# K and V of the first head on GpSimd's queue, ahead of the zero fills, in a decode step with its gradients

## The chip, the cores and the metric

The kernel runs on one core of one Trainium2 chip. Its time is the device time in microseconds (us). A kernel's time is the median of several executions, with the fastest and the slowest in brackets. Each trace is of one profiled execution, and its span is that execution's length.

## The reference, cut to what matters

One token goes through a layer norm, an attention over the last 4096 positions of a cache of 32768, and a gated block. Then the gradients of all inputs are taken.

```python
# x [1,1,448]; k_cache, v_cache [1,8,32768,256]; wq [448,4096]; wo [4096,448]; all bf16
W = 4096                                      # only the last W cache rows take part
k = repeat(k_cache[:, :, Sk - W:, :], 2)      # 16 query heads on 8 cache heads
v = repeat(v_cache[:, :, Sk - W:, :], 2)
p = softmax((q @ k.T) * Dh ** -0.5);  o = p @ v
h  = x + o @ wo
h2 = h + (layernorm(h) @ w_gate * (layernorm(h) @ w_up)) @ w_down
# results: h2 and the gradients of x, k_cache, v_cache, wq, wo, w_gate, w_up, w_down
```

The gradients of the two caches are what costs. Each is 134 MB, and seven eighths of both are zeros, which have to be written.

## The kernel before

Three things go on beside each other. GpSimd's queue (q0 in the profile) writes zeros from a buffer of 16 KB per partition, in fills of 2.1 MB. SyncE's queue (q1) brings most weights and the K and V rows of each head, and takes the results away; ScalarE's (q10, 1.61 MB in all) brings the up weights of the block. The engines compute attention, then the block, then the gradients.

`LD` is SyncE's queue, `ZQ` is GpSimd's.

```python
zeros = ar(0, ZW)                                # ZW = 8192 elements in each partition
...
nc.vector.memset(ar(0, ZW // 2), 0.0)            # L96: VectorE clears the first half,
nc.gpsimd.memset(ar(ZW // 2, ZW // 2), 0.0)      # L97: GpSimd the second
...
LD.dma_start(out=wqA, in_=wq_A)                  # query weights, 3.67 MB with the next line
LD.dma_start(out=wqB, in_=wq_B)
LD.dma_start(out=x_bf[:], in_=A_x.rearrange("a b d -> (a b) d"))
...
send_fills(0, HALF0)                             # the first 42 fills read all of zeros
send_fills(HALF0, HALF1, True)                   # 15 more read only its first half
...
load_kv(K_off[0], A_k_cache, 0)                  # all on LD, 2.1 MB each
LD.dma_start(out=dh2_bc[:], in_=grad_out...)
load_kv(V_off[0], A_v_cache, 0)
load_kv(K_off[1], A_k_cache, 1)
load_kv(V_off[1], A_v_cache, 1)
```

The block is worked through in three parts of 640, 512 and 640 columns. Part 2's gate and up weights lie in the second half of `zeros`, so they can't be loaded before the first 42 fills have been read out. When part 2 is done, that half is cleared again and the remaining fills are issued. I call this the **refill**.

```python
wgu_off = [RB + 28 * KB, ZW // 2]                # parts 1 and 3 | part 2, in the second half of zeros
...
for n in range(len(BLOCKS)):
    ...                                          # gate, up, down of part n
    if n + 2 < len(BLOCKS):
        load_block(n + 2)
    if n == 1:
        nc.vector.memset(ar(ZW // 2, ZW // 2), 0.0)   # L443
        send_fills(HALF1, len(fills) - 1)             # the refill
...
late_jobs = [(out_2, G - 1, 5, 7, 2 * ZW), (out_3, G - 1, 0, 6, 2 * ZW), (out_3, G - 1, 6, 7, ZW)]
# SyncE's own zero fills, issued behind the last gradients' stores
```

## Time and profile before

| of the profiled execution | before |
|---|---|
| median time, before the change was tried | 793.55 us (793.19 to 794.0, 3 runs) |
| span | 791.1 us |
| bytes moved | 334.75 MB, on average 423 GB/s |
| busiest compute engine | PE, 60% of the span |
| first fill issued, then first packets of q0 | 5.13 us, then 10.82 us |
| attention's last head done, refill issued, last SyncE stores issued | about 314, 383.3 and 742.9 us |

How to read it: the bytes over the plateau rate set a floor, and what comes on top are holes, stretches in which the DMA engines moved less than the plateau rate. The last row gives places where compute hands work to the queues. If compute were the bound, moving those times would move the end. The prediction shows the lines of the page, the windows and the first microseconds. These are the lines of the stage with the refill, from the timeline (start in us, duration, engine, line, operation, and in brackets the idle time before and what ended it):

```profile
315.62 0.38 SPq L366 DMA_DIRECT2D arena<-in_B_w_gate_dram  x1
...
353.05 1.50 PE L420 MATMUL gu_ps<-X_b,arena 128*128 128x1 bf16 x18 [2.59 <-DMA arena<-in_B_w_up_dram]
...
370.39 0.28 PE L420 MATMUL gu_ps<-X_b,arena 128*128 128x1 bf16 x3 [8.03 <-DMA arena<-in_B_w_gate_dram]
...
383.29 5.71 POOL L142 DMA_DIRECT2D out_dram<-arena  x6 [30.72 <-DVE arena L443]
...
742.93 0.95 SPq L661 DMA_DIRECT2D out_dram<-arena  x2
```

Part 2's gate weights are issued at 315.62, and PE's gate and up matmuls of part 2 run from 350.25 to 356.4 us, most of them from 353.05 on. The line at 370.39 is part 3, after 8 us of waiting for part 3's gate weights, which were issued at 355.36. The refill goes out at 383.29, for which GpSimd (POOL) had waited 30.7 us. VectorE had waited too: its last step of part 2 (376.07) stands behind its first step of part 3 (375.63). The last pair of the gradients' stores is issued at 742.93.

### The profile page before, as it was taken

To read this page: it belongs to the slowest core of one execution; us is meant where nothing else is said; L and a number is where in the kernel's file an instruction comes from. 1 tells how busy PE (TensorE), PEld (TensorE's weight loads), DVE (VectorE), ACT (ScalarE), POOL (GpSimd) and SP (SyncE) were. 2 spreads that over 40 slices of the span, in tenths; PEclk is the share of its full clock that TensorE was granted. 3 is DMA by queue.
4 is the path that set the end of the run, shared out by engine and by line. 5 is a ranking of instruction groups with operands and counts; after the bars stand their busy time and mean duration, and the time that the engine had idled before them with its cause. 6 is when DMAs were issued, how large, how long until landed. Compare 5 with 4: busy or idle time off the path is not lost.

```text
span 791.1 us, 7239 instructions
## 1 busy us (share of the span) xinstructions
PE 475.9 (60%) x2926; PEld 220.8 (28%) x2926; DVE 410.6 (52%) x621; ACT 196.1 (25%) x309; POOL 29.8 (4%) x41
## 2 busy tenths in 40 slices
PE   0359998999999999453226848583551535363100
PEld 0224333344343433142114714231210211131000
DVE  2105764847658476052884288486680583555300
ACT  0043123141241301000101207372331344134300
POOL 6000000000000000110300000000000000001000
PEclk9987999999999999655556959886556556556555
DMA  9999999999999999999999999999999999999998
GB/s 345 429 432 430 429 430 431 432 431 432 428 427 430 427 427 426 418 420 422 433 431 425 425 425 432 427 429 430 427 426 429 428 427 429 423 428 407 413 439 350
DMA packets 28759, 334.75 MB, mean 423 GB/s; under 512 B 1966, under 2 KB 5046, under 8 KB 6966
## 3 DMA queue, kind: packets, MB, share of 16 engines
q0 software_dynamic: 15904, 216.01, 64.2%
q1 hardware_dynamic: 11382, 116.68, 35.1%
q10 hardware_dynamic: 1440, 1.61, 0.6%
q8 instruction: 23, 0.38, 0.2%
q14 instruction: 10, 0.08, 0.0%
HBM read 53.69 MB, written 280.59 MB: 423 GB/s over the span
## 4 chain that ended last, share of the span: by engine, by line
another core or an unknown queue 40%; DMA 25%; DVE 14%; PE 10%; issue 2%; POOL 2%; ACT 1%; DVEq 0%; ACTq 0%; SPq 0%; POOLq 0%
DMA out_dram<-arena 25%; DVE arena L469 2%; PE rows_ps L266 2%; DVE arena L658 2%; DVE arena L554 2%; PE dqb_ps L512 2%; DVE arena L659 2%; PE d_ps L651 2%; PE tr_ps L263 1%; DVE arena L524 1%; DVE arena L438 1%; POOL out_dram L138 1%; PE dqb_ps L515 1%; DVE arena L623 1%
## 5 line engine op out<-in xcount | busy, mean ns | idle before, releaser
L322 DVE TENSOR_TENSOR arena<-arena,p_f 128x2048 bf16<-128x2048 bf16 x64 | 145.4, 2287 | 64.3 <-PE M_ps L327 64.2
L327 PE MATMUL M_ps<-arena 128*128 128x512 bf16 x512 | 129.3, 381 | 0.2 <-ACT arena L333 0.2
L651 PE MATMUL d_ps<-arena 32*128 32x512 bf16 x256 | 45.4, 521 | 100.6 <-DVE arena L659 85.7
L263 PE MATMUL tr_ps<-ident_bf,arena 128*128 128x128 bf16 x1024 | 92.2, 241 | 20.2 <-DMA arena<-in_A_k_cache_dram 12.7
L266 PE MATMUL rows_ps<-arena,vpad 128*16 128x512 bf16 x256 | 89.5, 445 | 21.4 <-DVE arena L623 15.9
L263 PEld LDWEIGHTS <-arena 128*128 128x128 bf16 x1024 | 68.3, 107 | 74.2 <-issue 60.3
L280 ACT COPY arena<-tr_ps 128x1024 bf16<-128x1024 bf16 x64 | 61.8, 1015 | 70.5 <-PE tr_ps L263 70.5
L330 PE MATMUL ok_ps<-arena 128*16 128x512 bf16 x256 | 64.0, 381 | 0.9 <-DVE arena L307 0.9
L655 ACT CAST arena<-d_ps 128x512 bf16<-128x512 f32 x64 | 37.7, 589 | 106.1 <-PE d_ps L651 106.1
L327 PEld LDWEIGHTS <-arena 128*128 128x128 bf16 x512 | 43.3, 99 | 59.2 <-issue 23.4
L621 ACT COPY arena<-tr_ps 128x1024 bf16<-128x1024 bf16 x32 | 32.5, 1016 | 109.9 <-PE tr_ps L263 35.8
L658 DVE CAST arena<-d_ps 128x512 bf16<-128x512 f32 x64 | 43.9, 686 | 18.2 <-PE d_ps L651 17.7
L659 DVE CAST arena<-d_ps 128x512 bf16<-128x512 f32 x64 | 43.6, 681 | 15.5 <-DMA out_dram<-arena 15.5
L651 PEld LDWEIGHTS <-arena 32*128 32x128 bf16 x256 | 10.7, 96 | 126.0 <-issue 81.9
L656 ACT CAST arena<-d_ps 128x512 bf16<-128x512 f32 x64 | 38.1, 595 | 16.8 <-DMA out_dram<-arena 16.8
L266 PEld LDWEIGHTS <-vpad 128*16 128x16 bf16 x256 | 18.7, 91 | 58.4 <-issue 50.6
L330 PEld LDWEIGHTS <-arena 128*16 128x16 bf16 x256 | 19.1, 89 | 41.6 <-issue 20.5
L549 DVE TENSOR_SCALAR arena<-arena,xT 128x1792 bf16<-128x1792 bf16 (+1 forms) x9 | 7.7, 881 | 37.1 <-DMA out_dram<-arena 37.1
L295 ACT ACTIVATE e_f<-cols_ps,nbias 128x32 f32<-128x32 f32 x16 | 4.5, 286 | 86.9 <-DVE nbias L291 86.9
L524 DVE CUSTOM_DVE_ANT_0 arena<-arena 128x4096 bf16<-128x4096 bf16 x3 | 13.1, 4421 | 23.7 <-ACT arena L517 23.7
L268 DVE COPY arena<-rows_ps 16x512 f32<-16x512 f32 x16 | 10.8, 676 | 27.7 <-PE rows_ps L266 27.7
L623 DVE COPY arena<-tr_ps 128x1024 bf16<-128x1024 bf16 x32 | 21.8, 683 | 3.0 <-PE tr_ps L263 2.5
(198 smaller groups left out, 382.2 us busy)
## 6 DMA issues: line engine op xcount, KB each, us to landing
out_dram<-arena POOLq DMA_DIRECT2D x11, 14336.0 KB, 196.1
out_dram<-arena SPq DMA_DIRECT2D x18, 2048.0 KB, 25.6
out_dram<-arena POOLq DMA_DIRECT2D x15, 2048.0 KB, 54.2
arena<-in_A_v_cache_dram SPq DMA_DIRECT2D x10, 2048.0 KB, 52.8
arena<-in_A_k_cache_dram SPq DMA_DIRECT2D x8, 2048.0 KB, 31.3
out_dram<-arena SPq DMA_DIRECT2D x4, 4096.0 KB, 26.1
out_dram<-arena POOLq DMA_DIRECT2D x1, 12288.0 KB, 43.0
out_dram<-arena POOLq DMA_DIRECT2D x1, 8192.0 KB, 337.3
```

Source lines behind the costliest of these rows:

```text
L263: nc.tensor.transpose(tr_ps[:, dh, i, :], X_sb[:, 4 * q + i, dh * 128:(dh + 1) * 128], ident_bf[:])
L266: nc.tensor.matmul(rows_ps[:], lhsT=pad[:, dh, 16 * q:16 * q + 16], rhs=XT[:, dh].rearrange("p t k -> p (t k)"), start=(q == 0 and dh == 0 ...
L280: sT_ps = dots(kv_at(K_off[g]), KT_slot, vpad[g % 2], rows1, ps_c, "cols", lambda q, XT, ps: nc.scalar.copy(out=XT, in_=ps))
L322: nc.vector.tensor_tensor(out=pK, in0=K_sb[:, 4 * c:4 * c + 4, :].unsqueeze(2).to_broadcast([128, 4, 2, Dh]), in1=p_f[:, c::8, :].unsqueez ...
L327: nc.tensor.matmul(M_ps[:, vh, :], lhsT=V_sb[:, t, vh * 128:(vh + 1) * 128], rhs=pK[:, i, :, :].rearrange("p h d -> p (h d)"), start=(t == ...
L330: nc.tensor.matmul(ok_ps[:].rearrange("p k d -> p (k d)"), lhsT=ppad[g % 2][:, 8 * (t % 4) + t // 4, :], rhs=both(g, t), start=(g == 0 and ...
L621: nc.scalar.copy(out=XT, in_=ps)
L651: nc.tensor.matmul(d_ps[:, qi].rearrange("p w d -> p (w d)"), lhsT=rTm[32 * q:32 * (q + 1), l, :], rhs=R_sb[32 * q:32 * (q + 1), :], start ...
L655: nc.scalar.copy(out=stV[:, t:t + 2, :], in_=d_ps[:, :, 0, :])
L656: nc.scalar.copy(out=stK[:, t:t + 2, :], in_=d_ps[:, :, 1, :])
L658: nc.vector.tensor_copy(out=stV[:, t:t + 2, :], in_=d_ps[:, :, 0, :])
L659: nc.vector.tensor_copy(out=stK[:, t:t + 2, :], in_=d_ps[:, :, 1, :])
```

## The change

Its intent: GpSimd's queue lies idle while the zeros are cleared. If it carries K and V of the first head in that time, they no longer stand behind the query weights in SyncE's queue, nor ahead of head 1's K and V, and attention can start earlier. GpSimd must not clear zeros then, so VectorE clears both halves.

```diff
-    nc.vector.memset(ar(0, ZW // 2), 0.0)
-    nc.gpsimd.memset(ar(ZW // 2, ZW // 2), 0.0)
+    def load_kv(eng, off, cache, g):
+        eng.dma_start(out=kv_at(off), in_=cache[0, g, Sk - W:, :].rearrange("(p t) d -> p t d", t=T))
+
+    load_kv(ZQ, K_off[0], A_k_cache, 0)
+    load_kv(ZQ, V_off[0], A_v_cache, 0)
+    nc.vector.memset(zeros, 0.0)
...
-    load_kv(K_off[0], A_k_cache, 0)
     LD.dma_start(out=dh2_bc[:], in_=grad_out.rearrange("a b d -> (a b) d").to_broadcast([128, D]))
-    load_kv(V_off[0], A_v_cache, 0)
-    load_kv(K_off[1], A_k_cache, 1)
-    load_kv(V_off[1], A_v_cache, 1)
+    load_kv(LD, K_off[1], A_k_cache, 1)
+    load_kv(LD, V_off[1], A_v_cache, 1)
# ... every other load_kv gets LD as its first argument, and stays where it was
```

More of the change, by code (lines that the diff above doesn't have):

```diff
@@ L204, in layernorm_bwd @@
         return r
-    def load_kv(off, cache, g):
-        LD.dma_start(out=kv_at(off), in_=cache[0, g, Sk - W:, :].rearrange("(p t) d -> p t d", t=T))
-    load_kv(K_off[0], A_k_cache, 0)
     LD.dma_start(out=dh2_bc[:], in_=grad_out.rearrange("a b d -> (a b) d").to_broadcast([128, D]))
-    load_kv(V_off[0], A_v_cache, 0)
-    load_kv(K_off[1], A_k_cache, 1)
-    load_kv(V_off[1], A_v_cache, 1)
+    load_kv(LD, K_off[1], A_k_cache, 1)
+    load_kv(LD, V_off[1], A_v_cache, 1)
     dup = small.tile([1, 128], bf16, tag="dup", bufs=1)
@@ L237 @@
     nc.vector.tensor_copy(out=qT_bf[:], in_=qT_ps[:])
-    load_kv(K_off[2], A_k_cache, 2)
-    load_kv(V_off[2], A_v_cache, 2)
+    load_kv(LD, K_off[2], A_k_cache, 2)
+    load_kv(LD, V_off[2], A_v_cache, 2)
     pT_all = const.tile([128, G, T, 2], bf16)
@@ L347 @@
                 if kind == "K":
-                    load_kv(K_off[n], A_k_cache, n)
+                    load_kv(LD, K_off[n], A_k_cache, n)
                 else:
-                    load_kv(V_off[n], A_v_cache, n)
+                    load_kv(LD, V_off[n], A_v_cache, n)
             if g == G - 2:
@@ L518 @@
         for g in range(2):
-            load_kv(MB + 16 * KB * g, A_v_cache, g)
+            load_kv(LD, MB + 16 * KB * g, A_v_cache, g)
         HJ = H * Dh // 2
```

## The prediction

> **What bounds the kernel now.** I read the page's slices first, to see whether any engine or the DMA is full all the time. The digits are tenths of busy time in 40 slices of 19.8 us, then GB/s; q0 is the queue that GpSimd issues on, q1 that of SyncE.
>
> ```profile
> PE   0359998999999999453226848583551535363100
> DVE  2105764847658476052884288486680583555300
> DMA  9999999999999999999999999999999999999998
> GB/s 345 429 432 430 429 430 431 432 431 432 428 427 430 427 427 426 418 420 422 433 431 425 425 425 432 427 429 430 427 426 429 428 427 429 423 428 407 413 439 350
> ...
> q0 software_dynamic: 15904, 216.01, 64.2%
> q1 hardware_dynamic: 11382, 116.68, 35.1%
> ...
> HBM read 53.69 MB, written 280.59 MB: 423 GB/s over the span
> ```
>
> No compute engine is full except PE in slices 4 to 15. The DMA is full everywhere, and only the first slice, the last and two near slice 37 are visibly under the plateau. So the kernel is bound by moving 334.75 MB, nearly all of it zeros being written to the two cache gradients. At 432 GB/s, the rate of the window from 11 to 20 us below, those bytes take 334.75 / 0.432 = 775 us. The span is 791.1 us, so everything that is not plain streaming, at the start, at the end and in between, is 16 us in sum. That is the whole pot a reordering of transfers can win from: a gain of 2% (15.9 us) would need all of it.
>
> Then I read where these 16 us lie, in the windows view (last two columns: DMA share and GB/s; the first is the window).
>
> ```profile
> 2.00:4.00 2.00, 0.00 (x0) 0.00 (x0) 1.99 (x10) 0.03 (x1) 2.00 (x1) 1.00 0.82 262
> 4.00:8.00 4.00, 0.37 (x1) 0.09 (x1) 1.80 (x9) 0.00 (x0) 3.95 (x8) 1.00 1.02 422
> 8.00:11.00 3.00, 0.00 (x0) 0.00 (x0) 0.00 (x0) 0.00 (x0) 3.00 (x4) 1.00 0.93 243
> 11.00:20.00 9.00, 0.00 (x0) 0.00 (x0) 0.00 (x0) 0.00 (x0) 1.64 (x3) 1.00 1.01 432
> 742.00:744.00 2.00, 0.14 (x4) 0.00 (x0) 1.29 (x2) 1.07 (x2) 0.00 (x0) 0.50 0.80 331
> ```
>
> Lost against 432: about 2 us before anything flows; 2 x 170/432 = 0.8 us in 2 to 4; 3 x 189/432 = 1.3 us in 8 to 11; 2 x 101/432 = 0.5 us in 742 to 744. The rest is scattered (rates of 418 to 425 in slices 17 to 24) or is the end.
>
> Third, when GpSimd's queue starts to move anything: the timeline of the engines that clear the zeros, and the DMA queues within a window (packets, MB).
>
> ```profile
> 0.74 3.51 POOL L97 MEMSET arena<- 128x4096 bf16 x1 [0.29 <-POOLq L694]
> 5.13 6.07 POOL L142 DMA_DIRECT2D out_dram<-arena  x6
> 11.19 1.45 POOL L138 DMA_DIRECT2D out_dram<-arena  x2
> 71.02 0.68 POOL L138 DMA_DIRECT2D out_dram<-arena  x1 [58.38 <-DMA out_dram<-arena]
> ...
> 1.25 1.76 DVE L96 MEMSET arena<- 128x2048 uint32 x1 [1.25 <-PEq L694]
> ```
>
> ```profile
> q1 hardware_dynamic: 238, 1.95, 96.2%
> q0 software_dynamic: 3, 0.05, 1.9%
> ```
>
> The second fence is 5 to 11 us: q0 moved three packets, although its first fill was issued at 5.13. From 11 to 13 us it moved 41. So q0 begins about 6 us after its first issue, and until then q1 carries the query weights alone.
>
> Last, what the compute chain waits for at the start, in the waits of 20 to 60 us and the timeline:
>
> ```profile
> PE ps L171 <- DMA x_bf<-in_A_x_dram: 14.7, 1, 14.7
> ...
> DVE pad L223 <- DMA dh_bc<-in_grad_out_dram: 10.1, 1, 10.1
> ...
> 58.48 1.78 PE L263 MATMUL tr_ps<-ident_bf,arena 128*128 128x128 bf16 x15 [4.97 <-DMA arena<-in_A_k_cache_dram]
> ```
>
> PE waits for x (behind the weights) until 21.0, for K of head 0 until 32.2, for the output gradient until 37.9, for K of head 1 until 58.5; after that attention runs on to about 314.
>
> **What the Trainium skill says.** "DMA: Bandwidth & Descriptors", section "Issuing engines are not separate DMA queues": DMAs of all issuers run on the same 16 engines and interleave, and using more issuers saves only issue time. The trace agrees: 432 GB/s from two queues in 11 to 20 us, 422 from one in 4 to 8. The same page, "Queues, rings and completion order": an engine takes turns between queues at packet granularity. The trace agrees roughly: where both have large rows each queue gets half. "VectorE: DVE Perf Modes", section "Zero memsets can be issued as uint32 (trn2)": one cycle per element whatever the type, so zeros go as 4-byte elements. The trace shows it: 4096 bf16 as 2048 uint32 in 1.76 us, against 3.51 us on GpSimd. "SBUF — State Buffer", section "Who interferes with whom": a VectorE instruction outside the 2-port modes with at most one SBUF input doesn't contend with GpSimd. The memsets of before overlapped (1.25 to 3.01 beside 0.74 to 4.25); whether GpSimd's descriptor writing is left alone too, no run here shows yet.
>
> **The change part by part.**
> Zero clearing: VectorE's memset doubles, 2 x 1.76 = 3.5 us, from 1.25 to about 4.8. GpSimd loses 3.51 us and gains two DMA issues of about 0.7 us (the 2 MB issues at L138 take 0.68), so its two identities (0.9 us in sum) are done near 3.2. Then the first fill waits for the memset until 4.8: 5.13 becomes about 4.9. Off the bound, worth 0.2 us at most.
> Queue order: K and V of head 0 (2 x 2.10 MB) go from q1 to the head of q0. Bytes removed: none. Issued at about 0.75 and 1.5 and with the 6 us delay measured above, q0 starts at about 6.5 instead of 11.1, and the fills start behind 4.2 MB of loads.
> Compute: in q1 the weights (3.67 MB, packets of 8 and 4 KB against 16 KB of q0) share from 6.5 instead of 11 us, so x and q come about 4 us later, near 31. But K and V are there, and the output gradient and K of head 1 follow directly. K of head 1: 4.2 MB fewer in front at some 210 GB/s is 20 us earlier, less the 4 us of slower weights, so near 41. Scores of head 0 take 17 us (38 to 54 before), so 31 to 48, and head 1's start near 46 instead of 58.5. Attention, the block after it and the gradients can thus run up to 12 us ahead, perhaps 8 in the later stages, where stores queue behind fills.
> What that is worth: little. The work before each stage goes faster, but the bytes queue on the same engines. Compute 8 to 12 us ahead means that q1 has carried more at a given time and q0 less; the fills then last longer beside the last stores. Before, q0 was empty by 733 and q1 alone carried the last 23 MB. Afterwards the two end closer together, at the same total.
> Sum: start, of 1.3 us in 8 to 11 I take half, 0.6, because the dip may come with the starting queue and only move to 4 to 7 us; earlier fill, 0.1; ramp in 2 to 4 us, nothing, as q0 isn't there yet; the hole at 742 filled by remaining fills, 0.5; other holes of 710 to 750, 0.3. In all 1.5 us: 793.55 - 1.5 = **792.0 us**.
>
> **Rivals.**
> A, compute was the path: the 12 us head start comes through, 793.5 - 12 = 781. For it: the last stores and late fills (SyncE's) are issued only after the last gradient stage, at 743. Against: DMA digit 9 in all slices; ending at 781 would need 430 GB/s with hardly a loss.
> B, the fills become the end: q0 gets 4.2 MB more, the split between the queues was tuned, and q0 finishes later. If all of it came out unhidden, 4.2/0.432 = 9.7 us more: 803. Against: q0 was empty 58 us before the end, far more than it gains; its limit of transfers in flight is untouched too: the third 2 MB fill waits for the first large one at 71.02, eight issues earlier, and two loads more in front only make the first two such fills wait for K and V.
> C, a new wait: the gradients of the block overwrite half of the zeros, so compute that is early can be held until the first 42 fills have landed, which the loads ahead delay by bytes moved out of q1; that sum is the same at 305. It would eat the head start, not add time: 793 to 794. A quarter of the chances lies here or with a start dip that only moves.
>
> **Range and chances.** The bytes set a floor near 779 (775 plus the 2 us before any flow and 2 at the end), and I see no idle DMA that the change could open wider than a few us. The noise of before is 0.8 us. I take **788.5 to 795.0** as the range. Faster by over 2% means under 777.7, below the floor: 0.01. Slower by over 2% means 809.4, with some stall that I haven't seen: 0.015. Within 2%: 0.975.
>
> **What would show it.** Right: DMA digits and the plateau as before, 334.75 MB again, q0's first packets near 6.5 us, x later than 21 us, head 1's transposes near 46 instead of 58.5, the last gradient stage ending before 743, q0 not empty at 733, and no DMA dip there. Wrong: the mean rate moves by more than 0.5%; q0's first packets come after 8 us; a slice in the middle drops under 400 GB/s because GpSimd waits longer; or a stretch at the end with only some of the engines working.

## The result, and the profile after

The kernel after took **794.03 us** (793.64 to 794.31, 4 runs), against 793.49 us (793.19 to 794.0, 4 runs) of before in the same rounds. The ratio is 1.0006, with a 95% interval from 0.9988 to 1.0023: the same. Ratios here are the mean time of one kernel's fast runs over that of the other's of the same rounds, so not quite the ratio of the medians quoted beside them. The span of the profiled execution was 792.0 us.

The page after, its lines of rates (40 slices) and of queues (packets, MB, share):

```profile
GB/s 358 401 430 432 428 432 428 432 429 430 432 428 429 429 421 413 426 423 422 430 432 418 427 419 431 428 429 427 427 427 428 429 427 428 421 429 408 420 441 356
...
q0 software_dynamic: 16192, 220.20, 65.7%
q1 hardware_dynamic: 11094, 112.48, 33.8%
```

4.2 MB moved from q1 to q0, and the sum is what it was. The first slice gained 13 GB/s, and the second, 19.8 to 39.6 us, lost 28. So what the start won was given back at once. The windows of after (the last two columns are DMA share and GB/s) show where:

```profile
8.00:11.00 3.00, 0.00 (x0) 0.00 (x0) 0.00 (x0) 0.00 (x0) 3.00 (x4) 1.00 0.96 410
...
18.00:22.00 4.00, 0.00 (x0) 0.00 (x0) 0.00 (x0) 0.00 (x0) 0.00 (x0) 1.00 1.03 291
...
742.00:744.00 2.00, 0.61 (x4) 0.11 (x4) 1.29 (x3) 1.07 (x2) 0.00 (x0) 0.50 0.91 386
```

The dip of 8 to 11 us is gone (243 before, 410 now), but 18 to 22 us has one of 291 GB/s. It costs 4 x (432 - 291)/432 = 1.3 us, as much as the old one. The packets of the first fill come at 21.5 us, at the end of the new dip. Before, they came at 10.82, at the end of the old one. In neither dip are the engines idle for long: the DMA share is 0.93 in the old one and 1.03 in the new. The packets take longer. In before, q1's packets of 8 KB took 1.023 x 16 x 4 us / 206 = 0.32 us each in 4 to 8 us and 0.896 x 16 x 3 us / 83 = 0.52 us in 8 to 11 (share of q1, 16 engines, window, packets). The hole at 742 shrank from 331 to 386 GB/s, worth 2 x 55/432 = 0.25 us.

The start, in the timeline of after:

```profile
1.29 0.70 POOL L97 DMA_DIRECT2D arena<-in_A_k_cache_dram  x1 [0.84 <-POOLq L693]
...
1.67 3.47 DVE L101 MEMSET arena<- 128x4096 uint32 x1 [1.67 <-PEq L693]
...
5.44 5.82 POOL L146 DMA_DIRECT2D out_dram<-arena  x6 [1.95 <-DVE arena L101]
...
27.86 0.21 DVE L215 COPY dup<-x_bf 1x128 bf16<-1x128 bf16 x1 [21.47 <-DMA x_bf<-in_A_x_dram]
...
48.03 0.68 PE L262 MATMUL tr_ps<-ident_bf,arena 128*128 128x128 bf16 x9
```

K of head 0 is issued at 1.29 and V at 2.00. The whole memset takes VectorE 3.47 us, and the first fill is issued at 5.44 after waiting 1.95 us for it. x is there at 27.9 (21.0 before). A head has 64 transposes; the first of the nine at 48.03 is the 64th, so head 1's start at 48.1 instead of 58.5. The same 5 to 11 us by queues (packets, MB, share of packet time), in which q0 had moved three packets before:

```profile
q0 software_dynamic: 95, 1.56, 62.0%
q1 hardware_dynamic: 121, 0.99, 39.4%
```

So compute did get ahead. VectorE's multiplies for attention's moments (products of K and V weighted by p, behind a head's softmax) began at 56.2 us instead of 61.5, and the last ones ran at 292.4 instead of 304.8, which is 12.4 us earlier. The lead grew on the way: 9.1 us at the first multiplies of head 1 (81.1 against 90.2), 9.6 at head 2's, 12.4 at head 3's. The last step is a wait of PE for K, 2.72 us, which ended at 130.50 in before and has no counterpart in after. But now the refill's stage, in the timeline of after:

```profile
346.18 1.23 SPq L365 DMA_DIRECT2D arena<-in_B_w_gate_dram  x1
...
369.72 0.41 PE L419 MATMUL gu_ps<-X_b,arena 128*128 128x1 bf16 x3 [30.55 <-DMA arena<-in_B_w_gate_dram]
...
385.36 5.65 POOL L146 DMA_DIRECT2D out_dram<-arena  x6 [31.81 <-DVE arena L442]
...
743.53 1.58 SPq L660 DMA_DIRECT2D out_dram<-arena  x2
```

PE waits 30.55 us for part 2's weights and gets to them at 369.72, 19 us later than before (350.25). Part 3 now follows at once, at 377.97 (370.39 before). The whole lead has become a wait: the refill is even 2 us later, and the last stores are 0.6 us later. The two traces differ in the order of SyncE's issues. Before, part 2's gate weights were issued at 315.62 and 321.82, ahead of part 3's. After, the build put part 3's loads first in SyncE's and ScalarE's queues, and part 2's gate weights went out at 346.18. Part 3's loads wait until part 1's buffer is free (344.08 us), and part 2's stand behind them.

### The profile page after: what moved, and what is told of

Read it like the earlier page. It is cut to its first block, busy times and chain, and to the rows that moved or that the text cites. A ratio compares the mean times of both kernels' runs of the same rounds, so it can differ in the third digit from the quotient of the medians.

```text
span 792.0 us, 7213 instructions
## 1 busy us (share of the span) xinstructions
PE 469.9 (59%) x2903; PEld 219.1 (28%) x2926; DVE 411.9 (52%) x621; ACT 196.2 (25%) x309; POOL 27.1 (3%) x42
## 2 busy tenths in 40 slices
DMA packets 28760, 334.75 MB, mean 423 GB/s; under 512 B 1967, under 2 KB 5047, under 8 KB 6967
## 4 chain that ended last, share of the span: by engine, by line
another core or an unknown queue 39%; DMA 27%; DVE 14%; PE 9%; issue 2%; ACT 1%; POOL 1%; DVEq 0%; ACTq 0%; SPq 0%; POOLq 0%
DMA out_dram<-arena 25%; DMA arena<-in_A_v_cache_dram 3%; DVE arena L468 2%; DVE arena L657 2%; PE dqb_ps L511 2%; DVE arena L553 2%; PE rows_ps L265 2%; DVE arena L658 2%; PE d_ps L650 2%; PE tr_ps L262 1%; DVE arena L523 1%; DVE arena L437 1%; DVE arena L622 1%; PE dqb_ps L514 1%
## 5 line engine op out<-in xcount | busy, mean ns | idle before, releaser
L326 PE MATMUL M_ps<-arena 128*128 128x512 bf16 x489 | 125.7, 380 | 1.8 <-issue 0.8
L262 PE MATMUL tr_ps<-ident_bf,arena 128*128 128x128 bf16 x1024 | 90.5, 237 | 20.2 <-DMA arena<-in_A_k_cache_dram 14.2
L419 PE MATMUL gu_ps<-X_b,arena 128*128 128x1 bf16 x112 | 9.7, 186 | 33.0 <-DMA arena<-in_B_w_gate_dram 32.0
## 6 DMA issues: line engine op xcount, KB each, us to landing
out_dram<-arena POOLq DMA_DIRECT2D x15, 2048.0 KB, 47.9
```

The source lines that it names most:

```text
L262: nc.tensor.transpose(tr_ps[:, dh, i, :], X_sb[:, 4 * q + i, dh * 128:(dh + 1) * 128], ident_bf[:])
L326: nc.tensor.matmul(M_ps[:, vh, :], lhsT=V_sb[:, t, vh * 128:(vh + 1) * 128], rhs=pK[:, i, :, :].rearrange("p h d -> p (h d)"), start=(t == ...
```

## The experiments

The two theories at this point:

- **Bytes**: the time is the bytes over the plateau rate plus the holes. A lead of compute is worth nothing, and a lag costs only where it opens a hole. The start's hole moved with the first fill.
- **Lost lead** (the prediction's rival A, with a reason why it didn't show): compute was on the path, and the swapped loads alone hid the gain. With the order kept, some 11 us should appear.

### order_kept: the lead without the swapped loads

Against after, the build is told to issue part 2's gate and up loads ahead of part 3's loads. This adds an order and no wait.

```diff
+            block_loads[n, i] = (d1, d2)         # the two loads of gate or up of part n
+            if n == 2:
+                for d in (d1, d2):
+                    for e in block_loads[1, i]:
+                        after_of(d, e)            # order only; likewise for part 3's w_down
```

> The changed kernel, with SyncE's and ScalarE's loads of the block's second part put back ahead of those of its third part, as in the kernel before (the changed kernel's build had swapped them, and PE then waited 30.6 us for the second part). If bytes bound the kernel: the 12 us head start of attention now comes through, the memset that gives the zeros back ends near 375 instead of 385 us, the last gradient stage ends 5 to 10 us before 743.5, and the time stays at 793.5 within 1.5 us. If compute was the path and only the swapped loads ate its head start: 782 to 786 us.

Measured: correct, 793.8 us (793.07 to 794.27, 5 runs), against 793.4 of before (792.64 to 793.96, 9 runs); ratio 1.0003, from 0.999 to 1.0015. Its timeline:

```profile
371.23 2.77 POOL L146 DMA_DIRECT2D out_dram<-arena  x3 [17.84 <-DVE arena L456]
...
732.39 1.63 SPq L674 DMA_DIRECT2D out_dram<-arena  x2
```

The lead now comes through to the end of compute: the refill 14 us earlier than in after (371.23 against 385.36), the last stores 11 us earlier (732.39 against 743.53). The time doesn't move. The hole at 742 to 744 us is closed as well (416 GB/s, against 331 in before), which shows no gain above the scatter either. This settles two things. The swapped loads were what ate the lead, and the lead is worth nothing. "Lost lead" falls, and rival A with it.

### fewer_bytes: what a byte costs

Against before, the first of SyncE's late fills into the last head, 4.19 MB, is left out. The result is wrong (one output isn't fully written).

```diff
-    late_jobs = [..., (out_3, G - 1, 0, 6, 2 * ZW), ...]
+    late_jobs = [..., (out_3, G - 1, 2, 6, 2 * ZW), ...]
```

> The kernel before without the first 4.19 MB of SyncE's late fills (a wrong result on purpose: that part of the output is left unwritten). If bytes bound the kernel: 4.19 MB / 0.432 GB/ms = 9.7 us less, so 783.8 within 1 us. If the chain of compute and its stores sets the end: less than 3 us of gain.

Measured: 783.46 us (783.2 to 783.54, 4 runs), ratio 0.9873, from 0.986 to 0.9887. Its page:

```profile
HBM read 53.69 MB, written 276.40 MB: 422 GB/s over the span
```

4.19 MB fewer take 793.4 - 783.46 = 9.9 us off, which is 4.19/9.9 = 0.42 MB per us, the mean rate of the kernel. Bytes come out of the time at full price. These fills are the last thing issued, behind the gradients' stores, so leaving them out would shorten the end under "lost lead" too; the expectation of under 3 us for that case was mistaken. It is order_kept, not this run, that tells the theories apart.

### x_late: compute later, a first try

Against before, the load of x goes behind V of head 0. No byte is added.

```diff
-    LD.dma_start(out=x_bf[:], in_=A_x.rearrange("a b d -> (a b) d"))
     ...
     load_kv(V_off[0], A_v_cache, 0)
+    LD.dma_start(out=x_bf[:], in_=A_x.rearrange("a b d -> (a b) d"))
```

> The kernel before, with the load of x moved behind K, the output gradient and V of head 0 in SyncE's queue, so that compute starts late on purpose: x near 48 us instead of 21, head 1's transposes near 67 instead of 58.5, everything behind them some 8 us later. If bytes bound the kernel: 793.5 within 1.5 us, as the fills still come back before the 2 MB ones run out near 396. If the compute chain sets the end: 801 to 802.

Measured: correct, 793.55 us (793.25 to 793.98, 4 runs), ratio 1.0, from 0.9984 to 1.0015. x came at 47.9 us instead of 21.0, and the first multiplies of the moments at 70.2 instead of 61.5, but the last ones at 305.0 (304.8 before). Attention caught up: PE's two waits for K in before, 7.7 us together between 55 and 160 us, are absent here. So this was a weak test: the lag was gone before it reached the refill.

### x_mid and x_later: compute later, so that it stays late

The same edit, with x behind K of head 1 (x_mid) and behind V of head 1 (x_later).

```diff
-    LD.dma_start(out=x_bf[:], in_=A_x.rearrange("a b d -> (a b) d"))
     ...
     load_kv(K_off[1], A_k_cache, 1)
+    LD.dma_start(out=x_bf[:], in_=A_x.rearrange("a b d -> (a b) d"))     # x_mid
     load_kv(V_off[1], A_v_cache, 1)
+    LD.dma_start(out=x_bf[:], in_=A_x.rearrange("a b d -> (a b) d"))     # x_later, instead
```

> The kernel before with x loaded behind K of head 1. In x_late the moments began 8.7 us later (70.2 instead of 61.5) but ended at the same 305, so attention took up the delay and that run said little of the later stages. Here x comes near 58 and attention should end 8 to 10 us later than before (near 323), the memset that gives the zeros back near 392 instead of 383. If bytes bound the kernel: 793.5 within 2 us, as the last 2 MB fills, issued near 352 and 44 us or more in flight, run out only near 398. If the compute chain sets the end: 801 to 804.

Measured for x_mid: correct, 799.58 us (798.13 to 800.62, 4 runs), against 793.43 (792.83 to 793.92, 7 runs); ratio 1.0073, from 1.0056 to 1.0089. I had expected no loss here, as I took the fills to last until 398 us. That was a miss. Its timeline and windows:

```profile
396.00 6.46 POOL L141 DMA_DIRECT2D out_dram<-arena  x7 [43.29 <-DVE arena L443]
```

```profile
391.00:396.00 5.00, 0.00 (x0) 0.00 (x0) 4.58 (x9) 0.00 (x0) 0.00 (x0) 0.50 0.24 102
396.00:401.00 5.00, 3.02 (x15) 1.57 (x16) 4.76 (x16) 1.01 (x1) 5.00 (x6) 0.50 0.78 303
```

The refill is issued at 396.00, and its first packets come at 397.40. The queues run dry from 391 on. Against 431 GB/s the two windows lose 5 x 329/431 = 3.8 us and 5 x 128/431 = 1.5 us, together 5.3 us. The kernel lost 6.1 us, and the profiled execution, the slowest of the four at 800.62, 7.2 us; the rest isn't located.

> The kernel before with x loaded behind V of head 1: x near 68, attention ends about 18 us later than before, the memset that gives the zeros back near 400. Then the 2 MB fills run out before it and the DMA has nothing but a few loads for some us. If bytes bound the kernel, only that hole costs time: 794 to 803, as many us more as the windows of 390 to 410 us lack against 430 GB/s. If the compute chain sets the end: 18 us more, 811.

Measured for x_later: correct, 808.88 us (808.53 to 809.36, 4 runs), ratio 1.0196, from 1.0181 to 1.0211. Its timeline and windows:

```profile
404.66 6.47 POOL L141 DMA_DIRECT2D out_dram<-arena  x7 [56.58 <-DVE arena L443]
```

```profile
391.00:396.00 5.00, 2.69 (x31) 2.39 (x31) 0.00 (x0) 0.00 (x0) 0.00 (x0) 0.50 0.38 154
396.00:401.00 5.00, 0.96 (x12) 0.81 (x11) 3.73 (x8) 0.00 (x0) 0.00 (x0) 0.50 0.01 3
401.00:406.00 5.00, 1.01 (x3) 0.34 (x4) 4.55 (x10) 0.00 (x0) 1.34 (x2) 0.50 0.00 0
```

The hole is now 3.2 + 5.0 + 5.0 = 13.2 us, of 15.4 us lost (15.9 by the profiled execution). The time lies outside both ranges that I had expected, above 794 to 803 and below 811: the windows explain most of the loss, not all. From x_mid to x_later the refill is 8.66 us later and the time 9.3 us longer (8.7 between the two profiled executions): behind the edge, a later refill comes out nearly one to one. Taken back on that slope, x_mid's 6.1 us put the edge near 396.0 - 6.1/(9.3/8.66) = 390.3 us, and its profiled 7.2 us near 389.

The edge also follows from the traces another way. GpSimd issues its last half-buffer fill at 351.88 us in before, and each issue waits until one eight issues earlier has landed. So some 8 x 2.1 MB were outstanding. At 0.43 MB per us that is an estimated 39 us of work, until about 391 (what other queues moved meanwhile is left out). This date is set by bytes, not by compute.

### act_queue: the two loads on a third queue

Against after, K and V of head 0 are issued by ScalarE.

```diff
-    load_kv(ZQ, K_off[0], A_k_cache, 0)
-    load_kv(ZQ, V_off[0], A_v_cache, 0)
+    load_kv(nc.scalar, K_off[0], A_k_cache, 0)
+    load_kv(nc.scalar, V_off[0], A_v_cache, 0)
```

> The changed kernel with K and V of head 0 issued by ScalarE instead of GpSimd, so on a third queue. The loads flow from 2 us on, the fills again start near 11 us, so if the dip belongs to the fills' start it lies in 8 to 11 us again; if it belongs to the weights' last third, it comes later, as the weights share their queue time. PE's first transposes come earlier than 14 us. If bytes bound the kernel: 793.5 within 1.5 us; if the compute head start counts, under 786.

Measured: correct, 795.68 us (795.0 to 796.22, 4 runs), against 793.5 of the same rounds; ratio 1.0027, from 1.0012 to 1.0042. Small, but clear of one, and outside the 1.5 us that I had expected. PE's first transposes came at 12.2 us, as expected. The dip was back at 8 to 11 us (344 GB/s), where the fills start again. x came at 39.2 us, 11 us later than in after. The price shows in the timeline and the window of the refill:

```profile
391.32 3.74 POOL L146 DMA_DIRECT2D out_dram<-arena  x4 [41.18 <-DVE arena L442]
```

```profile
391.00:396.00 5.00, 2.70 (x12) 1.25 (x13) 4.89 (x17) 1.01 (x1) 4.68 (x5) 0.50 0.73 285
```

The refill at 391.32 is just past the edge. This window loses 5 x 146/431 = 1.7 us and the one before it, at 378 GB/s, 0.6 us: 2.3 us, against 2.1 us measured (1.5 in the profiled execution, the fastest, whose dip at the start was 0.7 us smaller than before's). That the late refill is the cause rests on these windows and on x_mid and x_later; no run of act_queue with an earlier refill was made.

### loads_only and memset_only: the halves of the change

loads_only is after with the memset split as before; memset_only is before with VectorE clearing both halves.

```diff
-    nc.vector.memset(zeros, 0.0)
+    nc.vector.memset(ar(0, ZW // 2), 0.0)
+    nc.gpsimd.memset(ar(ZW // 2, ZW // 2), 0.0)      # loads_only; memset_only is the reverse, on before
```

> The changed kernel with the memset split as before (GpSimd clears its half after it has issued the two loads). GpSimd's memset of 3.5 us then runs from 2.6 to 6.1, identities until 7, first fill issued near 7.1 instead of 5.4. As K and V of head 0 keep GpSimd's queue busy until about 21 us, the fills start no later: 794 within 1 us, the same as the whole change. If the faster clearing is what matters, 1.7 us more than the changed kernel.

Measured: correct, 794.45 us (793.76 to 795.45, 4 runs), ratio 1.0013, from 0.9997 to 1.003. GpSimd's memset ran from 2.54 to 6.07 us behind its two issues, so the first fill was issued at 6.89. The dip came at 18 to 22 us, at 277 GB/s.

> The kernel before with VectorE alone clearing the zeros, the loads left where they were. The first fill is issued near 5.3 as before, its first packets come near 11: 793.5 within 1 us. If GpSimd's writing of descriptors is held up by VectorE's longer memset, the first packets come 1 us later or more.

Measured: correct, 794.59 us (792.76 to 795.24, 4 runs), ratio 1.001, from 0.9995 to 1.0025. Its window:

```profile
8.00:11.00 3.00, 0.00 (x0) 0.00 (x0) 0.00 (x0) 0.00 (x0) 3.00 (x4) 1.00 1.01 283
```

The first fill was issued at 5.46 instead of 5.13: VectorE was done at 1.67 + 3.47 = 5.14, and before, GpSimd's half had been done at 4.25. So clearing by VectorE alone is no gain by itself; it is what keeps the first fill from being issued at 6.9 once the loads stand ahead of it. As the fill's packets come at 21.6 us in loads_only and at 21.5 in after, behind the loads in both, that is worth nothing either. Neither half moves the time by more than the runs scatter. The dip stays at 8 to 11 us with the memset alone, and moves to 18 to 22 us with the loads.

### early_write and small_first: what the dip at the fills' start is

Two suspicions: that the first store of the kernel has a price, and that the first fill, of seven 2.1 MB pieces in one issue, is too large. Both runs are single looks on before, of unknown state, for the dip alone.

```diff
-    nc.vector.memset(ar(0, ZW // 2), 0.0)                        # early_write
+    nc.vector.memset(ar(0, 128), 0.0)
+    nc.scalar.dma_start(out=out_3[0, G - 1, 0:64, :]..., in_=ar(0, 128))     # 32 KB of zeros, at once
+    nc.vector.memset(ar(128, ZW // 2 - 128), 0.0)

-    send_fills(0, HALF0)                                          # small_first
+    send_fills(0, 1)
+    send_fills(1, GROUP)
+    send_fills(GROUP, HALF0)
```

> The kernel before with one small store more: 32 KB of zeros to a part of the output that is written again later, issued by ScalarE as soon as 128 columns are clear, near 2.5 us. The dip of the DMA rate lies in 8 to 11 us in the kernel before and in 18 to 22 us in the changed one, each time in the last 3 us ahead of the first large fill's packets. If the dip is the price of the very first store, it moves to 3 to 6 us and 8 to 11 us shows over 400 GB/s; if it belongs to the large fills' start, it stays in 8 to 11 at some 240. The time is 793.5 within 2 us in either case.

> The kernel before with its first large fill (14.7 MB) cut into one of 2.1 MB and one of 12.6 MB. If the dip ahead of the fills' first packets comes from the size of the first fill, 8 to 11 us shows over 350 GB/s and the first packets come sooner than 11 us; if it comes with any first fill, it stays at some 240 GB/s. The time is 793.5 within 2 us.

Measured: both correct; 794.01 us with the early store and 793.09 with the small first fill. The window of early_write, then that of small_first:

```profile
8.00:11.00 3.00, 0.00 (x0) 0.00 (x0) 0.00 (x0) 0.00 (x0) 3.00 (x4) 1.00 0.92 262
```

```profile
8.00:11.00 3.00, 0.00 (x0) 0.00 (x0) 0.00 (x0) 0.00 (x0) 3.00 (x4) 1.00 1.00 279
```

The dip stays in both, so neither suspicion holds. Nor is it the first use of GpSimd's queue: in after that queue starts with K at 5.65 us, and 8 to 11 us shows 410 GB/s. Nor is it the issuing of the large fills: GpSimd did that from 5.44 to 11.26 us in after, outside the dip. What the dip goes with in all these runs is the beginning of the zero fills on q0, wherever that is put. Its cause stays open.

## Why the prediction was right or wrong

The predicted time of 792.0 us stood beside 794.03 measured, inside the range of 788.5 to 795.0, and the time stayed within 2%.

**Right, and shown by an experiment:**

- *The bytes bound it.* The bytes and the plateau were as before, 4.19 MB fewer gave 9.9 us (fewer_bytes), and an earlier compute chain gave nothing (order_kept). One reading on the way was too strong: the bytes are not "nearly all" zeros. Seven eighths of the two cache gradients are 234.9 of 334.75 MB, 70%.
- *A head start of compute is worth little.* With the lead brought through to the last stores, 11 us earlier, the time was the same (order_kept). Rival A falls.
- *The fills don't become the end.* q0's last packet came at 732.3 us before and 732.4 after, although q0 had 4.2 MB more to move, so rival B falls. (That packet belongs to a last fill of 2.1 MB, which GpSimd issues at 714.97 and 715.77 after a wait for VectorE.)
- *The clearing is off the bound.* 3.47 us on VectorE against an estimate of 3.5, and no gain or loss alone that the runs could tell (memset_only). The prediction left open whether GpSimd's writing of descriptors is held up by the memset beside it: V's issue, wholly beside it, took 0.57 us, and issues of the same size with no memset beside them 0.67, so it wasn't.

**Right in number, by luck:** *attention 12 us ahead.* 12.4 measured at its end. The prediction had the whole 12 us at head 1's start (46 against 58.5). There it was 10.4 us, and 5.3 us at the first multiplies of the moments; the last 2.8 us came with a later wait for K that fell away (at 130.50 before), which the prediction hadn't counted.

**Wrong, by the steps of the sum.** It promised 1.5 us; measured was a loss of 0.5 us, within the scatter of the runs.

- *Start, half of the dip, 0.6 us.* The dip moved whole, as the prediction had feared, though to 18 to 22 us and not to 4 to 7. It follows the first fill, not the first packet of the queue. This term is zero.
- *Earlier fill, 0.1 us.* The first fill was issued at 5.44, 0.3 us later than before, and its packets came behind 4.2 MB of loads, at 21.5 us. The step took VectorE's memset to start at 1.25, as the shorter one had, and end by 4.8. It started at 1.67 and ended at 5.14.
- *The hole at 742, 0.5 us.* Half of it came, 0.25 us. The reason given for it failed: q0 was empty at 732.4, as before, so no fills were left to lie in that hole. With it failed three of the signs named for "right": q0 not empty at 733, no dip there (386 GB/s), and the last gradient stage ending before 743 (its stores were issued at 743.53).
- *Other holes, 0.3 us.* The three slices of 693 to 752 us were better by (429 + 408 + 420 - 428 - 407 - 413)/3 = 3 GB/s, over 59 us worth 0.4 us, of which the hole at 742 is 0.25. But 30 to 40 us fell from 427 to 414 GB/s (0.3 us) and 280 to 310 us from 425 to 416 (0.6 us).
- *Compute's times at the start.* q0 was put at 6.5 us and began at 5.65. Two errors partly cancel: K was issued at 1.29 and not 0.75, and the delay was 4.4 us and not the constant 6. x came 6.9 us later and not 4, and head 1's transposes began at 48.1, not near 46.
- *8 us ahead in the later stages.* Nothing was left at the refill (2 us later) and at the last stores (0.6 us later). Rival C had said that the head start could be eaten by the wait for the first 42 fills, and that the date of those fills is "the same at 305". GpSimd's issue that had waited 43 us for a landed fill came at 311.2 against 305.4, so that date wasn't constant, and in order_kept part 2's gate loads went out at 310.5. But what ate the lead was another thing that no part of the prediction had: the order of two loads in a queue, chosen by the build.

In all, rival C's outcome (793 to 794 us) came, by a mechanism that it didn't name. As the lead was worth nothing anyway, that error cost the prediction nothing. It matters for the slack: the refill must be out before about 390 us. Before sent it at 383.3, after at 385.4, order_kept at 371.2. So after has 2 us less to spare, and act_queue, past the edge, lost 2.1 us. The refill isn't the only date. The gradients' last stores come when q0 is empty and q1 alone feeds the engines, and there before has no slack: issued at 742.93, they leave 331 GB/s in 742 to 744 us. In x_late's profiled execution they were issued 0.8 us later (743.70), and that window fell to 202 GB/s.

No version here beats both kernels. What the runs point to is fewer bytes, above all the second reads of V of two heads and of the query weights, 4.19 + 3.67 = 7.9 MB or, at the rate of fewer_bytes, an estimated 19 us. I saw no free buffer to keep them in, so no version of it was tried, and the gain is argued only.

## What to carry to other kernels

When the DMA engines are full from the first microsecond to the last, work out the time as bytes over the plateau rate plus the holes, and ask of a reordering only which hole it closes and which it opens. Compute that feeds a full queue has a date, not a speed: ahead of it a lead is worth nothing, behind it each microsecond costs about one, so look up how long the outstanding transfers last (here to about 390 us, and again to 742) before calling an engine harmless. Look at the share of busy DMA engines and at the rate together: in the dips here the share was 0.93 and 1.03 at little more than half to two thirds of the rate. And after moving a transfer from one queue to another, compare the issue order of all queues in both traces, because the build may reorder loads far from the edited line.

## What the Trainium skill lacked or had wrong

- "DMA: Bandwidth & Descriptors", section "Specifications", gives a first-byte latency of about 1 us for GpSimd's path. Here the first packets came 4.4 us after the issue for K at the kernel's start (1.29 to 5.65) and 5.7 us for the first fill of before (5.13 to 10.82). In mid-kernel it was 1.4 us (396.00 to 397.40 in x_mid), near the page's figure. The page has no number for the start of a kernel.
- The same page, "Queues, rings and completion order", has an engine take turns between queues by packet. The traces agree: in 22 to 26 us of before, with large rows in both queues, each moved 52 packets and 0.85 MB. But the share of a queue then goes with the size of its packets: in 6 to 11 us of after, q0 moved 80 packets with 1.31 MB, and q1 87 with 0.71 MB. The page doesn't say what this does to a load that is waited for (x, 6.9 us later).
- No page has the dip that came just ahead of the first large fills' packets, to 243 GB/s in before and 291 in after, 1.3 us in each, with the packets taking longer and the engines hardly idle.
- No page warns that the build can swap the loads of two stages within a queue after an edit elsewhere. It cost PE a wait of 30.55 us here, and all of a lead of 12.4 us.
